# A fused recurrence and gated mixture on one core: 64-bit weights decoded with two VectorE instructions fewer, and the mixture's input splits queued a quarter step later

## The chip, the core and the metric

The kernel runs on one core of a Trainium2 chip. The core has TensorE (PE, matrix products; its weight loads are PEld), VectorE (DVE), ScalarE (ACT) and GpSimd (POOL), each with its own in-order queue, and SyncE (SP), whose queue issues nearly all of the DMAs here. The metric is the device time of one execution in microseconds (us). Times of before are those of three runs and of one profiled execution.

## What is computed

First a recurrence over 768 tokens, for 4 batches and 8 heads with a 40x40 state each; then a mixture over the tokens whose input is the recurrence's output.

```python
for t in range(S):
    y[:, :, t] = np.einsum('bhd,bhde->bhe', rt, state)
    Sa = np.einsum('bhde,bhe->bhd', state, at)
    state_decay = state * wt[:, :, None, :] - np.einsum('bhd,bhe->bhde', Sa, bt)
    state = state_decay + np.einsum('bhd,bhe->bhde', vt, kt)
...
h = np.maximum(x @ w_in, 0.0)
u, v = (h[..., :d_ff // 2], h[..., d_ff // 2:])
v_n = (v - mu) / np.sqrt(var + 1e-06)
v_s = np.einsum('ts,bsd->btd', w_spatial, v_n) + b_spatial[None, :, None]
gated = u * v_s
return (gated @ w_out).astype(np.float32)
```

The arrays `w_in` (320x1024) and `w_out` (512x320) come as 64-bit floats. Products are taken in a reduced fp32 format; to keep their accuracy, each operand is split into a high part and the rest, and three products replace one.

## The kernel before, in words

**Phase 1** is the recurrence in chunks of 64 tokens: two pairs of batches with 12 chunks each make 24 steps (NS = 24). A step handles 8 units in two groups g. Its chain is: `c_bp` (PE, from the state `Mc`) and its eviction on ACT, `c_ff` and its eviction, `c_xx` and its eviction (ACT, then two triangle selects on POOL), `c_mp` (PE) and `c_mp_out` (DVE, line 635), which writes the state for the next step; and `c_y` (PE) with `c_y_out` (DVE, line 659), which frees the PSUM bank that the next `c_bp` writes. Beside it run the preparation of later chunks (two scans and products on DVE, `b_...` products on PE with evictions on ACT and selects on POOL) and, for each group of four chunks, a triangular inversion on DVE in 33 slices (lines 368 and 372).

**The order is written by hand.** `at(t, fn)` puts a call into a list with a time in steps; the list is sorted by that time, then by the order of entry, and all calls before t = 24 are issued in that order. So on each engine the queue is in the order of t. Calls with t of 24 or more, and the whole of phase 2, are ordered by the compiler's planner, which estimates durations; `issue_after` keeps some of them behind marks in phase 1.

**Decoding.** `decode64_steps` (line 57) turns a 128-row tile of 64-bit floats, loaded as pairs of 32-bit words `lo` and `hi`, into the two fp32 parts `h` and `l`. Each `yield` ends a slice. Slice 0 loads; slices 1 to 7 are one DVE instruction each on the words (t[0], t[1], t[2] are three scratch tiles with one buffer each); slice 8 is a copy on ACT that makes `h`; slice 9 is two DVE instructions (lines 98 and 99). `w_in` makes six tiles of 128x512, decoded in steps 4 to 9: tile i has slice k at 4.2 + i + 0.1 k, its load 0.9 earlier (line 858). `w_out` makes four tiles of 128x320, decoded in the last part by `decode64` (line 149).

**The mixture's first half** starts when decoding is over: the decoding scratch is closed at 10.1 and its memory becomes that of the pool `act`. Twelve input tiles of 128 tokens follow, j = 0 to 11. `m_load` (DMAs on SP into the tile `xt`, one buffer), `m_split` (line 697: ACT copies `xt` to `xh`, 128x768; POOL subtracts twice, 128x512 and 64x256), then six products `m_u`/`m_v` in six of the slots of which each step from 11 on has four, at .22, .46, .65 and .80. Here own[0] is a tile's first slot; the tile's load stands at own[0] - 1.6 (10.12 for the first), its split at own[0] - 0.7. So the split of an even j stands at .52 of a step (10.52, 13.52, ...), that of an odd j at .95 (11.95, 14.95, ...).

**Neighbours in the order:** `b_lka_out` at .17 and .19, `c_ff_out` at .34 and .39, `b_l21_out` (line 482) at .54, `c_xx_out` at .60 and .65, `b_zt_out` at .68, `b_h_out` at .72 and .74, `c_mp_out` at .755 and .775, `b_x21_out` at .81, `c_y_out` at .90 and .94, the next step's `c_bp_out` at 1.04 and 1.09.

**Phase 2** is the product with `w_spatial` (lines 184 to 186), the gate (188, 189) and the output product (204). It begins inside the last part of phase 1.

Of the kernel before, what the change touches and what calls it, by code (L numbers as in the profile page):

```python
# [8 lines left out]
F32 = mybir.dt.float32  # L9
# [4 lines left out]
AF = mybir.ActivationFunctionType  # L14
ALU = mybir.AluOpType
# [14 lines left out]
NR = C + E  # L30
LATE = 2 * C
DH = 512

@with_exitstack
def tile_kernel(ctx, tc, early, late, vtok, win, wspT, bsp, wout, out):
    nc = tc.nc
    dram = ctx.enter_context(tc.tile_pool(name="dram", bufs=1, space=DRAM))
    B = out.shape[0]
    S = out.shape[1]
    xs = dram.tile([B, 2, NP, E, S], F32, name="xs")  # L40
    vns = dram.tile([B, S // P, P, DH], F32, name="vns")
    uts = dram.tile([B // NB, S // P, DH // P, P, NB, P], F32, name="uts")
    with ExitStack() as c1:
        marks = phase1(c1, tc, early, late, vtok, win, xs, vns, uts, dram)
    with ExitStack() as c2:
        phase2(c2, tc, marks, vns, uts, wspT, bsp, wout, out)


def split_hi(eng, hi, x):
    eng.activation(hi, x, AF.Copy)  # L50
# [6 lines left out]
def decode64_steps(nc, pool, h, l, src, n, bufs=1):  # L57
    raw = pool.tile([P, n], I64, name="d_raw", bufs=2)
    nc.sync.dma_start(out=raw, in_=src)
    yield  # L60
    words = raw.bitcast(I32).rearrange("p (n two) -> p n two", two=2)
    lo, hi = words[:, :, 0], words[:, :, 1]
    t = [pool.tile([P, n], I32, name=f"d_t{i}", bufs=bufs) for i in range(3)]
    nc.vector.tensor_scalar(
        out=t[0], in0=hi, scalar1=3, scalar2=0x7FFFFFFF,
        op0=ALU.logical_shift_left, op1=ALU.bitwise_and,
    )
    yield
    nc.vector.tensor_scalar(
        out=t[1], in0=hi, scalar1=-0x80000000, scalar2=0x40000000,  # L70
        op0=ALU.bitwise_and, op1=ALU.bitwise_xor,
    )
    yield
    nc.vector.tensor_tensor(out=t[0], in0=t[0], in1=t[1], op=ALU.bitwise_xor)
    yield
    nc.vector.tensor_scalar(
        out=t[1], in0=hi, scalar1=0x7FFFFFFF, scalar2=None, op0=ALU.bitwise_and
    )
    yield
    f1 = t[2].bitcast(F32)  # L80
    nc.vector.scalar_tensor_tensor(
        out=f1, in0=t[1], scalar=float(897 << 20), in1=t[0].bitcast(F32),
        op0=ALU.is_ge, op1=ALU.mult,
    )
    yield
    nc.vector.tensor_scalar(
        out=t[0], in0=t[2], scalar1=-0x800000, scalar2=None, op0=ALU.bitwise_and
    )
    yield
    f2 = t[1].bitcast(F32)  # L90
    nc.vector.scalar_tensor_tensor(
        out=f2, in0=lo.bitcast(U32), scalar=2.0 ** -52, in1=t[0].bitcast(F32),
        op0=ALU.mult, op1=ALU.mult,
    )
    yield
    split_hi(nc.scalar, h, f1)
    yield
    nc.vector.tensor_tensor(out=f1, in0=f1, in1=h.bitcast(F32), op=ALU.subtract)
    nc.vector.tensor_tensor(out=l, in0=f1, in1=f2, op=ALU.add)


def decode64(*args, **kw):
    for _ in decode64_steps(*args, **kw):
        pass


def phase2(ctx, tc, marks, vns, uts, wspT, bsp, wout, out):
    nc = tc.nc

    def behind(*keys):  # L110
        es = ExitStack()
        for key in keys:
            es.enter_context(tc.issue_after(marks[key]))
        return es
# [3 lines left out]
    TH = S // 2  # L118
    ND = DH // P

# [34 lines left out]
    def vload(b):  # L155
        vt[b] = []
        for i in range(NT):
            raw = wstg.tile([P, S], F32, name="raw", bufs=2)[:, 0:DH]
            nc.sync.dma_start(out=raw, in_=vns[b, i])
            vpool = vp[b % 2][i]  # L160
            h = vpool.tile([P, DH], F32R, name=f"vh{b % 2}{i}")
            l = vpool.tile([P, DH], F32R, name=f"vl{b % 2}{i}")
            with behind(("a", 23)):
# [59 lines left out]
def phase1(ctx, tc, early, late, vtok, win, xs, vns, uts, dscr):  # L223
    nc = tc.nc
# [452 lines left out]
    def decode(half, k):  # L677
        cs = slice(half * DH, (half + 1) * DH)
        yield from decode64_steps(nc, st["dec"], wh[:, k, cs], wl[:, k, cs], win[:, k, cs], DH)
# [92 lines left out]
    def at(t, fn, *args):  # L772
        plan.append((t, len(plan), fn, args))
# [60 lines left out]
    for q in range(GS, NS):  # L834
        t = PREP.get(q, q - 8 + 0.01)
# [18 lines left out]
    T_DEC, T_MOE = 4.2, 11  # L854
    for i in range(6):
        gen = decode(1 - i // 3, i % 3)
        for k in range(10):
            at(T_DEC + i + k * 0.10 - (0.9 if k == 0 else 0), step, gen)
    at(T_DEC + 5.9, open_act)
    slots = [T_MOE + k // 4 + (M1, M2, M3, M4)[k % 4] for k in range(3 * NS)]  # L860
# [1 line left out]
    def tail(t):  # L862
        return slots.index(t) if t >= NS else 0

    for j in range(NS // 2):
        bq, i = j // 6, j % 6
        own = slots[6 * j:6 * j + 6]
        at(max(own[0] - 1.6, 2 * j + 2.1, T_DEC + 5.92), m_load, bq, i)
        at(max(own[0] - 0.7, 2 * j + 2.7), m_split, bq, i)
        for t, d in zip((own[0], own[1], own[3], own[4]), range(DH // P)):  # L870
            at(t, m_u, d, bq, i, tail(t))
        for t, g in zip((own[2], own[5]), range(NB)):
            at(t, m_v, g, bq, i, tail(t))
            at(t + 0.14, m_n1, g)
            at(t + 0.42, m_root, g)
            at(t + 0.48, m_n2, g)
            at(t + 0.76, m_n3, g, bq, i)
# [12 lines left out]
    with tc.manual_schedule():  # L890
# [6 lines left out]
        for q in range(P // HB):  # L897
            rows = slice(q * HB, (q + 1) * HB)
            p.affine_select(
                out=maskl[rows], in_=maskl[rows], pattern=[[1, HB]], base=0,  # L900
# [10 lines left out]
        for m, val in ((maskp, 1.0), (maskn, -1.0)):  # L911
            p.memset(m, val)
            for rows in PR:
                p.affine_select(
                    out=m[rows], in_=m[rows], pattern=[[1, C]], base=0,
# [53 lines left out]
        while plan[n][0] < NS:  # L969
            t, _, fn, args = plan[n]  # L970
# [60 lines left out]
```

## Time and profile before

| what | us |
|---|---|
| three runs, median | 671.49 |
| three runs, lowest and highest | 670.7, 673.21 |
| the profiled execution | 672.68 |
| its span, first to last instruction | 671.0 |
| mean granted clock of TensorE, share of full | 0.936 |

The profile lists the execution of one core. "Busy" is the time in which an engine executes. A row of the time line gives start, duration, engine, line of the kernel, operation, output and inputs, count, and in brackets how long the engine had been idle and what released it. A row of the groups gives count, busy time in us, mean of one in ns and the idle time before them. The forty slices give busy tenths; PEclk is the clock that TensorE was granted, in tenths. A row of the windows gives the stretch, its length, the busy time and count of each engine, the granted clock, the share of the DMA engines and GB/s.

By the times of `c_y_out`, step 4 ends at 153.3, step 9 at 246.1, step 10 at 266.6 and step 23 at 496.3 us of the span.

### The profile page before, as it was taken

How to read it: one execution, taken by the hardware profiler on the slowest of the kernel's cores; microseconds unless marked ns; L12 is line 12 of the kernel's file. 1: busy time of each engine (PE TensorE's matmuls, PEld its weight loads, DVE VectorE, ACT ScalarE, POOL GpSimd, SP SyncE). 2: the span in 40 equal slices, each digit the busy share in tenths (PEclk: the TensorE clock that was granted, in tenths of full speed). 3: DMA queues.
4: the chain of work that ended last, by engine and by line, in shares of the span. 5: the costliest groups of instructions: out<-in, count | busy, mean ns of one | idle time of the engine just before them, and what ended most of it. 6: DMA issues, size and time to landing. Idle time of an engine off the chain costs nothing.

```text
span 671.0 us, 25860 instructions
## 1 busy us (share of the span) xinstructions
PE 577.4 (86%) x10960; PEld 522.7 (78%) x10960; DVE 454.1 (68%) x990; ACT 381.0 (57%) x850; POOL 226.5 (34%) x298
## 2 busy tenths in 40 slices
PE   1448784598777888999999999999989999999997
PEld 1347674487666776888888888888879899999997
DVE  7998689979999995878895676453285573322220
ACT  2136662367656665888878887888755552232212
POOL 6013340223232233334342242342243745352121
PEclk9977997679787786999999999999989999999999
DMA  8764866387555546656565256366286467150001
GB/s 190 115 117 66 144 148 136 69 175 147 129 127 122 129 108 125 132 136 170 138 189 153 76 156 168 89 172 162 83 234 191 152 184 231 48 169 30 30 30 59
DMA packets 106331, 87.68 MB, mean 131 GB/s; under 512 B 35496, under 2 KB 92072, under 8 KB 104296
## 3 DMA queue, kind: packets, MB, share of 16 engines
q1 hardware_dynamic: 105672, 84.31, 50.9%
q10 hardware_dynamic: 544, 1.72, 1.2%
q8 instruction: 86, 1.41, 1.0%
q14 instruction: 29, 0.24, 0.1%
HBM read 59.20 MB, written 20.50 MB: 119 GB/s over the span
## 4 chain that ended last, share of the span: by engine, by line
PE 42%; DVE 3%; ACT 2%; DMA 2%; issue 2%; POOL 1%; SPq 0%; ACTq 0%; POOLq 0%; DVEq 0%
PE po L204 6%; PE pg L186 4%; PE pg L185 4%; PE pv L764 4%; PE pg L184 4%; PE pv L717 4%; PE ch L586 2%; PE ch L568 2%; PE bp L550 2%; PE bp L646 1%; PE bk L434 1%; PE bk L456 1%; PE ch L624 1%; DMA vns<-vr 1%; PE bk L404 1%
## 5 line engine op out<-in xcount | busy, mean ns | idle before, releaser
L411 POOL TENSOR_SCALAR_AFFINE_SELECT Rt<-Rt 64x512 f32<-64x512 f32 (+1 forms) x144 | 83.9, 584 | 143.2 <-ACT Rt L597 115.3
L411 POOL TENSOR_SCALAR_AFFINE_SELECT At<-At 64x512 f32<-64x512 f32 x48 | 41.4, 862 | 157.8 <-ACT At L421 153.7
L560 ACT ACTIVATE Rt<-bp 64x416 f32<-64x416 f32 x96 | 49.1, 511 | 49.5 <-PE bp L550 47.8
L188 DVE TENSOR_TENSOR g<-pg,bb 128x384 f32<-128x384 f32 x32 | 17.7, 555 | 79.1 <-PE pg L186 69.5
L368 DVE TENSOR_TENSOR itmp<-A 128x30 f32<-128x30 f32 (+9 forms) x180 | 67.3, 374 | 3.2
L550 PE MATMUL bp<-lin,Mc 40*64 40x104 f32 x768 | 48.2, 284 | 21.7 <-DVE y L659 21.2
L184 PE MATMUL pg<-wsh,vh 128*128 128x384 f32 x192 | 65.0, 339 | 0.0
L185 PE MATMUL pg<-wsl,vh 128*128 128x384 f32 x192 | 65.0, 338 | 0.0
L186 PE MATMUL pg<-wsh,vl 128*128 128x384 f32 x192 | 63.2, 338 | 0.0
L372 DVE TENSOR_TENSOR A<-A,itmp 128x30 f32<-128x30 f32 (+9 forms) x180 | 59.0, 328 | 6.2
L550 PEld LDWEIGHTS bp<-lin,Mc 40*64 40x64 f32 x768 | 42.0, 155 | 24.7 <-DVE y L659 23.8
L54 POOL TENSOR_TENSOR gl<-g,gh 128x384 fp32r<-128x384 f32 x32 | 33.3, 1044 | 59.2 <-ACT gh L50 59.2
L597 ACT ACTIVATE Rt<-ch 64x416 f32<-64x416 f32 x96 | 49.1, 511 | 4.7 <-PE ch L586 2.4
L50 ACT ACTIVATE gh<-g 128x384 fp32r<-128x384 f32 x32 | 16.6, 521 | 53.5 <-DVE g L189 53.5
L568 PE MATMUL ch<-Rt,At 128*64 128x104 f32 x768 | 45.3, 276 | 1.8 <-issue 1.1
L344 PE MATMUL bk<-at,sl 64*32 64x32 f32 x1536 | 21.6, 206 | 26.9 <-DVE sl L329 20.7
L568 PEld LDWEIGHTS ch<-Rt,At 128*64 128x64 f32 x768 | 40.0, 152 | 5.8 <-issue 2.3
L586 PE MATMUL ch<-ffs,xf 64*64 64x104 f32 x768 | 42.2, 263 | 0.0
L344 PEld LDWEIGHTS bk<-at,sl 64*32 64x32 f32 x1536 | 18.2, 117 | 29.9 <-issue 14.7
L635 DVE TENSOR_TENSOR Mc<-ch,scn 104x160 f32<-104x160 f32 x44 | 18.4, 434 | 33.1 <-PE ch L624 20.6
L54 POOL TENSOR_TENSOR vl<-raw,vh 128x512 fp32r<-128x512 f32 x24 | 31.4, 1317 | 24.4 <-ACT vh L50 21.2
L586 PEld LDWEIGHTS ch<-ffs,xf 64*64 64x64 f32 x768 | 37.2, 140 | 1.1
(133 smaller groups left out, 1511.6 us busy)
## 6 DMA issues: line engine op xcount, KB each, us to landing
ein<-in_early SPq DMA_DIRECT2D x108, 129.0 KB
lin<-in_late SPq DMA_DIRECT2D x48, 160.0 KB
At<-at SPq DMA_DIRECT2D x48, 128.0 KB
uts<-ur SPq DMA_DIRECT2D x48, 128.0 KB
vns<-vr SPq DMA_DIRECT2D x24, 256.0 KB
raw<-vns SPq DMA_DIRECT2D x24, 256.0 KB
ut<-uts SPq DMA_DIRECT2D x24, 256.0 KB
Rt<-in_vtok SPq DMA_DIRECT2D x48, 80.0 KB
```

The costliest lines, as they stand in the source:

```text
L54: eng.tensor_tensor(out=lo, in0=x, in1=hi.bitcast(F32), op=ALU.subtract)
L184: nc.tensor.matmul(pg, lhsT=vh[:, dc], rhs=w_h, start=(i == 0), stop=False)
L185: nc.tensor.matmul(pg, lhsT=vh[:, dc], rhs=w_l, start=False, stop=False)
L186: nc.tensor.matmul(pg, lhsT=vl[:, dc], rhs=w_h, start=False, stop=(i == NT - 1))
L368: nc.vector.tensor_tensor(out=tp, in0=A[:, k + 1:, k:k + 1].broadcast_to([P, m, k]), in1=A[:, k:k + 1, 0:k].broadcast_to([P, m, k]), op=AL ...
L372: nc.vector.tensor_tensor(out=A[:, k + 1:, 0:k], in0=A[:, k + 1:, 0:k], in1=tp, op=ALU.add)
L411: nc.gpsimd.affine_select(out=t, in_=t, pattern=[[0, k], [1, C]], base=0, channel_multiplier=-1, compare_op=ALU.is_gt, fill=0.0,)
L550: nc.tensor.matmul(bp[PR[par], q, :], lhsT=Mc[RR[par], n, :], rhs=li[RR[par], n, C:], start=(q == 0), stop=False, skip_group_check=True,)
L560: nc.scalar.activation(Rt[par][PR[par], gp, :], st["bp", g][PR[par]], AF.Copy)
L568: nc.tensor.matmul(ff[PR[1 - par], q, :], lhsT=At[par][:, n, :], rhs=Rt[par][:, n, :], start=True, stop=True,)
L586: nc.tensor.matmul(xx[ev, q, :], lhsT=xf[ev, n, :], rhs=ffs[ev, q, :], start=True, stop=True,)
L597: done = nc.scalar.activation(Rt[par][PR[par], gp], xx[PR[1 - par]], AF.Copy, scale=-1.0)
```

## The change

In the decode, four instructions on the high word (shift and mask; keep and flip the sign and top exponent bits; combine; absolute value) become three: a shift and mask that also clears one bit more, a combined and-or on DVE, and an absolute value on ACT, taken of the word read as an fp32 number. The threshold of the comparison on line 82 is then an fp32 constant. DVE has seven instructions per tile instead of nine, ACT two instead of one. The absolute value shares slice 1 with the first DVE instruction, so that a tile has 8 slices instead of 10: the ACT copy is slice 6 instead of 8 (0.2 steps earlier), the closing pair slice 7 instead of 9. Second, every `m_split` stands at own[0] - 0.45 instead of own[0] - 0.7: at .77 of a step for even j, at .20 of the next for odd j.

```diff
+TINY = 1.125 * 2.0 ** -15
...
     nc.vector.tensor_scalar(
-        out=t[0], in0=hi, scalar1=3, scalar2=0x7FFFFFFF,
+        out=t[0], in0=hi, scalar1=3, scalar2=0x3FFFFFFF,
         op0=ALU.logical_shift_left, op1=ALU.bitwise_and,
     )
+    nc.scalar.activation(t[1].bitcast(F32), hi.bitcast(F32), AF.Abs)
     yield
-    nc.vector.tensor_scalar(
-        out=t[1], in0=hi, scalar1=-0x80000000, scalar2=0x40000000,
-        op0=ALU.bitwise_and, op1=ALU.bitwise_xor,
-    )
-    yield
-    nc.vector.tensor_tensor(out=t[0], in0=t[0], in1=t[1], op=ALU.bitwise_xor)
-    yield
-    nc.vector.tensor_scalar(
-        out=t[1], in0=hi, scalar1=0x7FFFFFFF, scalar2=None, op0=ALU.bitwise_and
+    nc.vector.scalar_tensor_tensor(
+        out=t[0], in0=hi, scalar=-0x40000000, in1=t[0], op0=ALU.bitwise_and, op1=ALU.bitwise_or,
     )
     yield
     f1 = t[2].bitcast(F32)
     nc.vector.scalar_tensor_tensor(
-        out=f1, in0=t[1], scalar=float(897 << 20), in1=t[0].bitcast(F32),
+        out=f1, in0=t[1].bitcast(F32), scalar=TINY, in1=t[0].bitcast(F32),
         op0=ALU.is_ge, op1=ALU.mult,
     )
...
         gen = decode(1 - i // 3, i % 3)
-        for k in range(10):
+        for k in range(8):
             at(T_DEC + i + k * 0.10 - (0.9 if k == 0 else 0), step, gen)
...
-        at(max(own[0] - 0.7, 2 * j + 2.7), m_split, bq, i)
+        at(max(own[0] - 0.45, 2 * j + 2.7), m_split, bq, i)
```

## The prediction

> **What bounds the kernel now.** I read the engines' busy line and the forty slices first, then the windows by stage, then the time line of VectorE (DVE) and of ScalarE (ACT) inside the stage that the change touches.
>
> ```profile
> DVE  7998689979999995878895676453285573322220
> ...
> PEclk9977997679787786999999999999989999999999
> ```
>
> A slice is 16.8 us, and the first is slice 0. TensorE (PE) is the busiest engine over the span, but the slices show stages: DVE has nine tenths or more from slice 9 to 14, and the granted clock of PE is mostly at 0.6 to 0.8 there and full later. All six decodes of the expansion weights lie in that part (steps 4 to 9). The windows by stage make it exact (length, then busy time of PE, PEld, DVE, ACT, POOL, granted clock, DMA share, GB/s):
>
> ```profile
> 143.65:257.54 113.89, 90.66 (x2469) 80.53 (x2468) 109.34 (x223) 74.33 (x169) 34.13 (x49) 0.88 0.58 130
> ...
> 257.54:267.10 9.56, 9.28 (x233) 7.92 (x234) 3.20 (x9) 5.23 (x12) 4.81 (x8) 0.50 0.87 140
> ...
> 257.54:484.00 226.46, 224.52 (x4965) 194.53 (x4966) 147.23 (x371) 179.69 (x404) 78.59 (x120) 0.98 0.54 140
> 484.00:545.00 61.00, 56.89 (x407) 51.99 (x404) 37.69 (x103) 33.91 (x73) 29.31 (x28) 0.97 0.60 182
> ```
>
> From 143.65 to 257.54 DVE is busy 109.34 of 113.89 us while ACT has 74.33. Then PE is busy for 224.52 of 226.46 us. So a microsecond taken from DVE before 257.5 should move everything behind it, and one taken later, nothing. DVE's time line shows where that run begins and ends:
>
> ```profile
> 143.19 0.42 DVE L354 TENSOR_TENSOR Lc<-bk,maskl 128x256 f32<-128x256 f32 x1 [2.17 <-PE bk L344]
> ...
> 149.20 0.45 DVE L635 TENSOR_TENSOR Mc<-ch,scn 104x160 f32<-104x160 f32 x1 [1.29 <-ACT Rt L597]
> 150.04 0.44 DVE L635 TENSOR_TENSOR Mc<-ch,scn 104x160 f32<-104x160 f32 x1 [0.40 <-PE ch L624]
> ...
> 262.02 0.44 DVE L635 TENSOR_TENSOR Mc<-ch,scn 104x160 f32<-104x160 f32 x1 [4.13 <-DMA Rt<-in_vtok]
> ```
>
> Between 150.04 and the 4.13 us of idle time before 262.02 no row of DVE has a wait in brackets: its queue is never empty for over 100 us.
>
> **Part 1: two DVE instructions fewer per decode (steps 4 to 9).** Lines 69, 74 and 76 go, one SCALAR_TENSOR_TENSOR over the same 128x512 words comes. In a full queue an instruction costs the time from its start to the next start; tile 1:
>
> ```profile
> 163.65 0.42 DVE L69 TENSOR_SCALAR d_t<-d_raw 128x512 int32<-128x512 int32 x1
> 163.99 0.58 DVE L368 TENSOR_TENSOR itmp<-A 128x210 f32<-128x210 f32 x1
> ...
> 164.90 0.69 DVE L74 TENSOR_TENSOR d_t<-d_t,d_t 128x512 int32<-128x512 int32 x1
> 165.50 0.84 DVE L368 TENSOR_TENSOR itmp<-A 128x220 f32<-128x220 f32 x1
> ...
> 166.68 0.45 DVE L76 TENSOR_SCALAR d_t<-d_raw 128x512 int32<-128x512 int32 x1
> 167.05 0.38 DVE L368 TENSOR_TENSOR itmp<-A 128x228 f32<-128x228 f32 x1
> ```
>
> Removed: 0.34 + 0.60 + 0.37 = 1.31 us. The new instruction is not in the trace; the nearest row is line 91's, of the same kind and size, which reads every other word as it will. The last row of this view is ScalarE's copy of the same tile, for later:
>
> ```profile
> L74 DVE TENSOR_TENSOR d_t<-d_t,d_t 128x512 int32<-128x512 int32 x6 | 4.3, 710 | 0.0
> ...
> L91 DVE SCALAR_TENSOR_TENSOR d_t<-d_raw,d_t 128x512 f32<-128x512 uint32 x6 | 4.1, 681 | 0.0
> ...
> L76 DVE TENSOR_SCALAR d_t<-d_raw 128x512 int32<-128x512 int32 x6 | 3.0, 497 | 0.0
> L69 DVE TENSOR_SCALAR d_t<-d_raw 128x512 int32<-128x512 int32 x6 | 2.8, 468 | 0.0
> ...
> L50 ACT ACTIVATE wh<-d_t 128x512 fp32r<-128x512 f32 x6 | 3.8, 630 | 4.1 <-DVE d_t L81 4.1
> ```
>
> It lasts 681 ns; less the 0.08 us or so by which an instruction overlaps the next (0.69 against 0.60 above) it is 0.61 us. Net per tile 0.70 us from below. By the means of the rows it is 468 + 710 + 497 - 681 = 994 ns. I take 0.8 for five tiles, 4.0. Tile 0 falls into step 4, where DVE still waits (the first three rows of its time line), so its removed instructions only lengthen those waits; but the generator is shorter, so two of its other instructions (lines 86 and 91, 0.34 + 0.60) now come ahead of the wait that ends at 149.20. I count 0.6. **Sum 4.6 us; bounds 3.5 (0.70, tile 0 at nothing) and 5.6 (0.994, tile 0 at 0.6).**
>
> The two bounds differ because some of the rows are stretched while GpSimd works. In step 20 this is plain: the TENSOR_SCALAR of line 76 over 128x320 words lasts 1.29 us beside a split's subtraction on POOL, and 0.33 where POOL is idle.
>
> ```profile
> 448.10 1.29 DVE L76 TENSOR_SCALAR d_t<-d_raw 128x320 int32<-128x320 int32 x1
> ...
> 489.99 0.33 DVE L76 TENSOR_SCALAR d_t<-d_raw 128x320 int32<-128x320 int32 x1
> ...
> 446.48 2.73 POOL L54 TENSOR_TENSOR xl<-xt,xh 128x512 fp32r<-128x512 f32 x1 [2.53 <-DMA Rt<-in_vtok]
> ```
>
> The Trainium skill, "SBUF — State Buffer", section "SBUF: two separate sides", says that VectorE and GpSimd share one port pair as an exclusive lock that whoever starts first holds for its whole instruction. The rows agree. By that rule the stretch is met by whichever DVE instruction comes next, the new one with two SBUF inputs too, so the removal would be worth the lower 0.70 per tile, and part 1 some 4.1 us.
>
> **What becomes late instead.** The steps' own chain is next: y (L659) of one step, through bp, ff, xx and the state product (L624), to DVE's L635 of the next.
>
> ```profile
> 227.49 0.41 DVE L659 TENSOR_TENSOR y<-bp,Et 104x256 f32<-104x256 f32 x1
> ...
> 239.79 0.51 PE L624 MATMUL ch<-tk,Rt 128*40 128x40 f32 x16
> ...
> 242.93 0.78 DVE L635 TENSOR_TENSOR Mc<-ch,scn 104x160 f32<-104x160 f32 x2
> ```
>
> From the end of the second y (227.90) the chain takes 12.4 us (to 240.30), DVE 15.0 (to 242.93). In the new order the closing pair (lines 98 and 99, 1.3 us) stands ahead of the second y instead of behind it, and line 91 ahead of L635: DVE's side becomes some 15.0 - 1.3 + 0.3 = 14.0, the chain's 12.4 plus the new ACT instruction. That leaves about 1 us per step: enough, but no more.
>
> **The absolute value on ScalarE.** It is queued in front of c_ff_out. Nothing shows it on this engine; the nearest row is the copy of the tile, 630 ns, and the DVE run leaves ACT 113.89 - 74.33 = 39.6 us idle, 6 us a step. I take 0.63 on ACT and nothing on the end; if the 1 us of slack were gone, 6 x 0.63 = 3.8 us. Behind it wait c_ff_out, tok_out and then PE's c_xx; ahead of it, its data (a DMA issued 0.9 steps earlier) and the previous tile's last use of the buffer (0.4 steps earlier) are done. The four output decodes, of 128x320 words, lie in the last part, where DVE is busy 37.69 and ACT 33.91 of 61.00 us: they save and cost nothing there by themselves.
>
> **Part 2: the split, 0.25 steps later.** Step 10 holds the first one:
>
> ```profile
> 252.93 1.13 ACT L781 ACTIVATE xf<-XT 128x256 f32<-128x256 f32 x3
> 256.43 0.84 ACT L50 ACTIVATE xh<-xt 128x768 fp32r<-128x768 f32 x1 [2.37 <-DMA xt<-xs]
> 257.30 0.78 ACT L482 ACTIVATE l<-bk 32x256 f32<-32x256 f32 x2
> 258.10 2.12 ACT L597 ACTIVATE Rt<-ch 64x416 f32<-64x416 f32 x4
> ...
> 253.41 1.64 PE L586 MATMUL ch<-ffs,xf 64*64 64x104 f32 x32
> 257.73 1.46 PE L492 MATMUL bk<-XT,l 32*32 32x32 f32 x32 [2.67 <-ACT l L482]
> ...
> 264.22 1.94 PE L646 MATMUL bp<-Rt,tk 128*40 128x64 f32 x32
> ...
> 237.15 2.12 ACT L597 ACTIVATE Rt<-ch 64x416 f32<-64x416 f32 x4
> ...
> 240.85 1.09 PE L646 MATMUL bp<-Rt,tk 128*40 128x64 f32 x32
> ```
>
> ACT is free at 254.06, waits 2.37 us for the input tile, copies it for 0.84, and only then evicts what PE has had ready since 255.05. At 10.77 instead of 10.52 the split stands behind c_xx_out, zt_out and h_out. L482 could start at 254.06: **3.2 us.** PE's 2.67 us of idle time goes with it, and that matters twice: the window from 257.54 to 267.10 runs at a granted clock of 0.50. In step 9, at full clock, the evictions' end (239.27) to c_y's end (241.94) takes 2.7 us; here 260.22 to 266.16, 5.9. If the clock stays up, another 3.2 us; in step 8 too an idle time of 2.5 us is followed by half clock:
>
> ```profile
> 226.99 2.52 PE L550 MATMUL bp<-lin,Mc 40*64 40x104 f32 x26 [2.53 <-DVE y L659]
> ...
> 228.00:230.00 2.00, 2.00 (x40) 0.50 0.62 150
> ```
>
> (The second row is a window of PE alone.) I take **2.0** (bounds 0 and 3.2).
>
> All twelve splits move, each one ACT and two POOL instructions, no DMA: on ACT past c_xx_out, zt_out and h_out or past c_bp_out and lka_out, on POOL past the triangle selects. The DMAs of the next input wait in SP's queue for the split's release, now 0.28 steps behind it instead of 0.53: about 4.9 us (226.46 us over 13 steps, 17.4 each). All eight POOL instructions of the window from 257.54, the split's two among them, take 4.81, so SP may wait a microsecond, and the input copies behind it with it. In the PE-bound stage only 226.46 - 224.52 = 1.9 us are there to win; I count 0, bounds a gain of 1.9 and a loss of 1. The tenth split leaves the order written by hand (23.95 becomes 24.20) and the four output decodes change, so the last part's order, which a planner makes, will change: 61.00 - 56.89 = 4.1 us of PE idle time are there to win and as much to lose; I count 0.
>
> **Sum:** 4.6 + 3.2 + 2.0 = 9.8 us. The profiled execution took 672.68 (span 671.0 and 1.7 around it), so 662.9; the three runs' median is 671.49, 1.2 below it, so **661.7 us**.
>
> **Rivals.** (1) *The new wait eats the old one's place*: the chain's slack is less than 1 us, steps 5 to 9 gain nothing and pay the 0.63 on ACT; the split's 3.2 + 2.0 remains: -5.2 + 3.8 = -1.4, 670.1. Against it: 12.4 against 14.0. Chance 0.10. The Trainium skill, "ScalarE: Activation LUTs", section "Rules for kernel authors", would have simple elementwise work on VectorE rather than ScalarE; by that rule this rival wins. The rows bear it out in size only (630 ns on ACT against 497 or less on DVE); DVE is the full engine here. (2) *The last part's new order gives back* 4 us: 665.7. For it: PE stands idle there now for 4.1 us. Chance 0.18. (3) *Slower: function tables.* The one load in the trace serves all 850 activations:
>
> ```profile
> L253 ACT ACT_TABLE_LOAD x1 | 1.3, 1283 | 1.4 <-PEq L1018 1.4
> ```
>
> Were the absolute value in another table, ten uses would bring twenty loads of 1.28 us, 25.7 us on ACT; less 6 us of slack in steps 4 to 9, and with 9.8 won, about +10: 681. It decides from eight loads on the path. Chance 0.04. The same page, section "Table sets: the hidden batching unit", lists abs among the cheap functions that every set holds; no row here shows it. (4) *More*: the clock stays up in steps 5 to 9 as well and the last part tightens, another 5 us: 656.5. Chance 0.08.
>
> **Numbers.** Forecast (657.5 to 665) 0.55, rival 2 with half successes up to 668 0.20, rival 1 and other small outcomes 0.13, rival 4 0.08, slower 0.04. A change below 0.5% (3.4 us) could not be told from none: faster 0.83, same 0.13, slower 0.04. The range, 655.5 to 669.0, spans from rival 4 to almost rival 1.
>
> **What would show it.** Right: the DVE run ends 4 to 5 us earlier (near 253); ACT's L482 of step 10 follows L781 without a wait; no half clock after it; PE's dense stage begins 8 to 11 us earlier and stays as long; one table load. Wrong: waits in brackets on L635 or L659 in steps 5 to 9, ACT idle for a function table, or a last part longer than 61 us.

## The result, and the profile after

| kernel | median, us | lowest, highest | runs | ratio to the kernel before, 95% interval |
|---|---|---|---|---|
| before | 671.49 | 670.46, 677.24 | 5 | |
| changed | 664.92 | 659.76, 670.56 | 5 | 0.9865 [0.9825, 0.9906] |

The change gains 6.6 us by the medians of all runs; the forecast was 9.8 (661.7 us). The ratio leaves out the slow run of the changed kernel (670.56) and stands for 9.1 us, with an interval from 6.3 to 11.8, so the five runs of each kernel don't tell the gain from the forecast. The profiled execution of the changed kernel took 665.08 us (span 663.3), 7.6 less than that of before.

Where the time went is read from `c_y_out`, whose second row in a step ends the step. The steps' lengths in the two profiles:

| stage | before | changed | difference |
|---|---|---|---|
| up to the end of step 3 (same instructions) | 135.5 | 134.2 | -1.3 |
| steps 4 to 9 | 110.6 | 107.6 | -3.0 |
| step 10 | 20.6 | 13.7 | -6.9 |
| step 11 | 16.3 | 22.4 | **+6.0** |
| steps 12 to 22 | 198.7 | 197.3 | -1.4 |
| step 23 and the rest | 189.3 | 188.2 | -1.1 |

Two stages gain as forecast in sign. Step 11 gives most of step 10's gain back.

The window of before from the end of step 3 to the end of step 9 (length, busy time of PE, PEld, DVE, ACT, POOL, granted clock, DMA share, GB/s):

```profile
135.46:246.07 110.61, 90.41 (x2502) 80.50 (x2502) 104.24 (x213) 72.08 (x163) 33.16 (x48) 0.87 0.60 133
```

The same of the changed kernel, then its step 10, and the dense stage behind step 11:

```profile
134.19:241.75 107.56, 88.48 (x2502) 78.29 (x2502) 101.72 (x203) 74.99 (x169) 34.12 (x48) 0.89 0.61 136
...
241.66:255.14 13.48, 12.63 (x401) 11.16 (x398) 12.93 (x29) 11.52 (x27) 5.50 (x9) 1.00 0.45 121
...
279.40:476.00 196.60, 195.66 (x4325) 169.69 (x4321) 127.89 (x332) 161.25 (x364) 67.77 (x104) 1.00 0.53 142
```

DVE's busy time falls by 2.5 us and so does the stage, by 3.0; ACT has 6 instructions and 2.9 us more. Step 10 runs at full clock. The dense stage of PE behind it stays dense: 195.66 of 196.60 us.

The groups of the changed kernel (count, busy us, mean ns, idle before):

```profile
L318 DVE TENSOR_TENSOR at<-ein,Et 128x512 f32<-128x512 f32 x7 | 6.6, 941 | 0.2
...
L71 DVE SCALAR_TENSOR_TENSOR d_t<-d_raw,d_t 128x512 int32<-128x512 int32 x6 | 4.1, 685 | 0.0
L65 DVE TENSOR_SCALAR d_t<-d_raw 128x512 int32<-128x512 int32 x6 | 3.4, 571 | 0.0
L81 DVE TENSOR_SCALAR d_t<-d_t 128x512 int32<-128x512 int32 x6 | 3.0, 498 | 0.0
...
L69 ACT ACTIVATE d_t<-d_raw 128x512 f32<-128x512 f32 x6 | 4.0, 674 | 0.0
...
L248 ACT ACT_TABLE_LOAD x1 | 1.3, 1283 | 1.4 <-PEq L1013 1.4
```

The new DVE instruction takes 685 ns (681 taken in the forecast), the absolute value 674 (630 taken), and there is still one table load. The same view of before has the rows of the same three instructions shorter (of line 64 only the mask has changed):

```profile
L323 DVE TENSOR_TENSOR at<-ein,Et 128x512 f32<-128x512 f32 x6 | 4.4, 735 | 0.2
...
L86 DVE TENSOR_SCALAR d_t<-d_t 128x512 int32<-128x512 int32 x6 | 2.7, 446 | 0.0
L64 DVE TENSOR_SCALAR d_t<-d_raw 128x512 int32<-128x512 int32 x6 | 2.5, 418 | 0.0
```

The time line of the changed kernel in step 10 and the start of step 11, ACT and PE:

```profile
247.21 1.13 ACT L776 ACTIVATE xf<-XT 128x256 f32<-128x256 f32 x3
248.36 0.78 ACT L477 ACTIVATE l<-bk 32x256 f32<-32x256 f32 x2
...
253.94 0.84 ACT L51 ACTIVATE xh<-xt 128x768 fp32r<-128x768 f32 x1 [0.78 <-issue]
...
261.99 0.58 PE L563 MATMUL ch<-Rt,At 128*64 128x104 f32 x2 [3.42 <-issue]
263.68 3.00 PE L563 MATMUL ch<-Rt,At 128*64 128x104 f32 x30 [1.12 <-DMA Rt<-in_vtok]
```

Line 477 follows line 776 at once: the wait for the input tile is gone. But 6.6 us after step 10 has ended (255.42), `c_ff` (line 563) is only beginning: PE stands for 3.42 and, after two products, for 1.12 us, the second time for `Rt<-in_vtok`, the token rows that `vtok_load` brings in two transfers (due at .48 and .62 of the step before). The bracket of the first wait names nothing, but it is the first transfer: the trace has the last updates of the two transfers' semaphores at 261.90 and 263.55 us, each 0.1 us before the products that follow. The clock pays too: over 264 to 266 us the window shows

```profile
264.00:266.00 2.00, 2.00 (x28) 2.00 (x25) 2.00 (x2) 0.52 (x1) 0.00 (x0) 0.50 0.45 120
```

a granted clock of 0.50 with PE busy throughout. The reason is in SP's queue, the same time line:

```profile
241.44 1.56 SPq L666 DMA_DIRECT2D xs<-y  x4
...
255.46 0.60 SPq L384 DMA_DIRECT2D Rt<-in_vtok  x1
...
257.08 0.58 SPq L384 DMA_DIRECT2D Rt<-in_vtok  x1
```

From the storing of step 9's output at 241.44 to the second issue of token rows at 257.08 SP works through 23 transfers, at about 0.6 us an issue, almost without a gap: 15.6 us. In before the list is as long, but step 10 took 20.6 us and `c_ff` of step 11 began 10.6 us after the issue:

```profile
245.76 1.57 SPq L671 DMA_DIRECT2D xs<-y  x4
...
260.02 0.57 SPq L389 DMA_DIRECT2D Rt<-in_vtok  x1
...
270.64 1.65 PE L568 MATMUL ch<-Rt,At 128*64 128x104 f32 x32
```

By the same semaphore the rows had landed there at 266.30, 4.3 us before their use. Now step 10 takes 13.7, less than the list, and PE asks for the rows some 1.5 us after their issue (it is out of other work at 258.57); they land 6.5 us after it, about as long as in before (6.3).

### The profile page after: what moved, and what is told of

Same layout as the page of the kernel before. It is cut to its first block, busy times and chain, and to the rows that moved or that the text cites. A ratio compares the mean times of both kernels' runs of the same rounds, so it can differ in the third digit from the quotient of the medians.

```text
span 663.3 us, 25848 instructions
## 1 busy us (share of the span) xinstructions
PE 571.8 (86%) x10960; PEld 518.3 (78%) x10960; DVE 448.4 (68%) x970; ACT 384.2 (58%) x860; POOL 225.9 (34%) x298
## 4 chain that ended last, share of the span: by engine, by line
PE 63%; DVE 15%; DMA 7%; issue 6%; ACT 4%; SPq 3%; POOL 1%; DVEq 0%; ACTq 0%; POOLq 0%
PE po L199 6%; PE pv L759 6%; PE pv L712 6%; PE pg L179 5%; PE pg L180 5%; PE pg L181 5%; PE ch L563 4%; PE bp L545 4%; PE ch L581 4%; PE bk L429 2%; DMA ein<-in_early 2%; DVE itmp L363 2%; PE bk L451 2%; PE bk L399 2%; PE bp L641 2%
## 5 line engine op out<-in xcount | busy, mean ns | idle before, releaser
L563 PE MATMUL ch<-Rt,At 128*64 128x104 f32 x768 | 48.0, 283 | 5.9 <-issue 4.8
L563 PEld LDWEIGHTS ch<-Rt,At 128*64 128x64 f32 x768 | 42.2, 157 | 10.4 <-issue 7.1
L339 PE MATMUL bk<-at,sl 64*32 64x32 f32 x1536 | 21.2, 203 | 26.5 <-DVE sl L324 20.7
L339 PEld LDWEIGHTS bk<-at,sl 64*32 64x32 f32 x1536 | 17.7, 114 | 29.5 <-issue 14.4
L179 PEld LDWEIGHTS pg<-wsh,vh 128*128 128x128 f32 x192 | 36.6, 190 | 2.4 <-ACT vh L51 2.2
L630 DVE TENSOR_TENSOR Mc<-ch,scn 104x160 f32<-104x160 f32 x44 | 18.5, 436 | 29.0 <-PE ch L619 18.7
```

Source lines behind the costliest of these rows:

```text
L179: nc.tensor.matmul(pg, lhsT=vh[:, dc], rhs=w_h, start=(i == 0), stop=False)
L563: nc.tensor.matmul(ff[PR[1 - par], q, :], lhsT=At[par][:, n, :], rhs=Rt[par][:, n, :], start=True, stop=True,)
```

## The experiments

The kernels ran in three groups, each group on one chip together with the kernel before, whose medians there were 670.33 us (split_only, decode_only, first_split, vtok_early), 673.07 (after_again, vtok_again, decode_again, abs_twice) and 672.63 (vtok_third, vtok_abs_dve, before_vtok, before_again). The stages of all profiles, in us, for the readings below:

| kernel | up to step 3 | steps 4-9 | step 10 | step 11 | 12-22 | 23 and rest |
|---|---|---|---|---|---|---|
| before | 135.5 | 110.6 | 20.6 | 16.3 | 198.7 | 189.3 |
| before_again | 136.5 | 110.6 | 20.7 | 16.3 | 199.2 | 188.1 |
| split_only | 136.9 | 111.6 | 15.2 | 17.3 | 196.4 | 189.7 |
| decode_only | 135.3 | 110.4 | 20.3 | 16.4 | 198.4 | 187.4 |
| decode_again | 135.9 | 110.2 | 21.2 | 16.3 | 198.3 | 188.1 |
| changed | 134.2 | 107.6 | 13.7 | 22.4 | 197.3 | 188.2 |
| after_again | 135.5 | 108.7 | 14.7 | 16.9 | 197.6 | 186.5 |
| abs_twice | 136.3 | 109.6 | 13.9 | 21.0 | 197.7 | 187.5 |
| first_split | 139.4 | 107.5 | 15.0 | 16.2 | 198.4 | 186.9 |
| vtok_early | 137.6 | 109.1 | 13.7 | 15.4 | 199.2 | 186.3 |
| vtok_again | 138.0 | 107.3 | 13.7 | 15.4 | 198.4 | 188.2 |
| vtok_third | 136.7 | 107.6 | 13.7 | 15.4 | 199.6 | 189.2 |
| vtok_abs_dve | 136.2 | 112.9 | 14.8 | 15.8 | 198.6 | 191.4 |
| before_vtok | 138.1 | 110.1 | 21.1 | 15.9 | 199.4 | 188.4 |

The first column is a measure of the scatter: nothing but the early token rows touches it, and it takes 134.2 to 139.4 us.

### Each part alone: split_only, decode_only, decode_again

The kernel before with the later splits only:

```diff
-        at(max(own[0] - 0.7, 2 * j + 2.7), m_split, bq, i)
+        at(max(own[0] - 0.45, 2 * j + 2.7), m_split, bq, i)
```

> The old nine-instruction decode with all splits 0.25 steps later. Theory (a new wait, step 11's token rows from the DMA queue, eats what step 10 wins): step 10, which took 20.6 us from the end of one y to the next and 13.7 with both changes, is held by VectorE's run to 257.5 and comes to 15 to 16; then the first product of step 11 waits some 2 us for the token rows, and the whole gains 3 to 5 us. Rival (the two parts are independent and add, the wait in step 11 belongs to the pair): step 10 falls by the full 6.9 us and the whole by 6 to 7.

Measured: 667.94 us (664.05 to 674.3, 12 runs), ratio 0.9955 [0.9936, 0.9974]. Step 10 falls by 5.4 us, to 15.2, as the theory said. Most of the rest of the way to 13.7 is the clock: at the start of the step PE had stood 3.87 us for the last y of step 9, as its time line shows, and the 26 products of line 550 take 2.52 us, where the next step has 1.38 for as many at full clock. In step 11 the second transfer of token rows is awaited for 0.82 us, not 2; the bracket names an eviction into `ur`, which `c_ff` doesn't read, but the last update of the rows' semaphore is at 268.52 us.

```profile
248.19 2.52 PE L550 MATMUL bp<-lin,Mc 40*64 40x104 f32 x26 [3.87 <-DVE y L659]
...
268.65 1.61 PE L568 MATMUL ch<-Rt,At 128*64 128x104 f32 x30 [0.82 <-ACT ur L766]
```

The whole gains 2.4 us by the medians and 3.0 by the ratio, about the lower end of the theory's 3 to 5; the rival's 6.9 and 6 to 7 us didn't come.

The changed kernel with the splits put back (0.45 to 0.7), that is, the shorter decoding alone:

> The new decode with the splits where they were. Theory: VectorE's run ends 3 to 4.5 us earlier; ScalarE still waits for the input tile in step 10, TensorE still idles and drops to half clock, step 10 stays at 19 to 21 us, and step 11 has no wait for token rows (about 16.3 us). Whole: 3 to 4.5 us faster than before. Rival (the decode's gain is the one that is eaten): less than 1.5 us. If the parts' gains add to more than the 6.6 us that both brought, they share a bound.

Measured: 668.46 us (665.72 to 673.5, 12 runs), ratio 0.9989 [0.9962, 1.0016]; steps 4 to 9 as long as before, step 10 still 20.3 us. The gain, 1.9 us by the medians and 0.7 by the ratio, is nearer to the rival's than to the theory's. Its step 5 held a wait of 3.21 us of PE; in most other profiles it is 0.6 to 2.2. So it ran again:

> The shorter decoding alone, once more. Theory A (the shorter decoding is worth 2 to 3 us in steps 6 to 9 by itself, and the 3.2 us in which TensorE stood in step 5 came from one execution): steps 4 to 9 take 107.2 to 108.6 us, step 10 still 20 us with ScalarE standing at the split, ratio to the kernel before 0.995 to 0.997. Theory B (a faster VectorE by itself runs into the loads of the early rows): step 5 takes over 20 us again and the ratio stays within 0.2% of 1.

Measured: 669.27 us (666.91 to 673.63, 12 runs), ratio 0.9946 [0.9915, 0.9977]. The ratio is near theory A's; steps 4 to 9, at 110.2 us, are not, and step 5 at 19.5 lies between: neither theory's numbers hold together. Up to step 10 this kernel's order is the changed kernel's on every engine, so that its 110.2 and 110.4 and the 107.5 to 108.7 of changed, after_again and first_split are one order's scatter. Its step 10 keeps the old wait and the half clock; ACT's row:

```profile
257.06 0.84 ACT L51 ACTIVATE xh<-xt 128x768 fp32r<-128x768 f32 x1 [3.27 <-DMA xt<-xs]
```

By the medians on the same chip the decoding alone gains 1.9 and 3.8 us and the split 2.4: together 4.3 to 6.2, with 6.6 and 7.9 for both at once (changed and after_again). By the ratios it is 0.7 and 3.6, 3.0, and 9.1 and 7.9. The parts add up to less than the pair each time; the intervals, 1.3 us and more to each side, neither show nor exclude that the pair gains more than its parts.

### The token rows earlier: vtok_early, vtok_again, vtok_third

The changed kernel with the token rows queued ahead of the input tile's loads:

```diff
-            at(q - 1 + 0.48 + 0.14 * par, vtok_load, q, par)
+            at(q - 1 + 0.03 + 0.01 * par, vtok_load, q, par)
```

> The changed kernel, with each step's token rows queued 0.45 to 0.58 steps earlier on SyncE, ahead of the mixture's input tiles. Theory: in step 11 the first product (c_ff) no longer waits (3.42 and 1.12 us) nor drops to half clock, step 11 falls from 22.4 to 16.5 to 17.5 us, and the whole gains 4 to 6 us on the changed kernel: about 659 to 661. Rival (the DMA engines, not the order of the queue, are full between 256 and 262 us, and another transfer is late instead): step 11 stays above 20 us and the whole gains less than 2.

> The changed kernel with the token rows queued 0.45 of a step earlier, once more beside the changed kernel. Theory A: steps 10 and 11 take 28.5 to 30 us together again, ratio to the kernel before 0.984 to 0.988, 0.4 to 0.7% below after_again. Theory B: as after_again within 0.2%.

> The changed kernel with the token rows queued 0.45 of a step earlier, as the base for vtok_abs_dve: 660.5 to 663.5 us, steps 4 to 9 in 107 to 109 us, steps 10 and 11 in 29.1 us together for the third time.

Measured: 661.44 us (659.97 to 663.01), 662.45 (660.68 to 664.64) and 663.31 (660.53 to 667.54), 6 runs each; ratios 0.9866 [0.984, 0.9892], 0.9851 [0.9812, 0.9891], 0.9844 [0.9793, 0.9894]. In all three profiles step 10 takes 13.7 and step 11 15.4, less than the theory's 16.5 to 17.5; the rival is dead. vtok_third's windows of the two steps:

```profile
244.28:257.94 13.66, 12.81 (x406) 11.34 (x403) 13.11 (x29) 11.39 (x26) 5.36 (x9) 1.00 0.52 131
257.94:273.35 15.41, 15.41 (x341) 13.67 (x337) 14.30 (x26) 10.68 (x24) 6.17 (x10) 1.00 0.73 141
```

PE is busy for all of step 11, at full clock. This is the fastest version, 8.9 to 10.6 us below the kernel before on the same chip. On the second chip it stands 2.7 us below the changed kernel (662.45 to 665.17), though the two intervals overlap. Not all of step 11 is gained: the table has 0.7 to 2.3 us more in steps 12 to 22 than for the changed kernel. Step 3 ended at 136.7 to 138.0 us (changed: 134.2 and 135.5), but without the early rows it ended as late in first_split.

### The changed kernel again: after_again

> The changed kernel as it is, once more. Theory A (the token rows' transfer is always the last thing to arrive in step 11, since step 10 is now shorter than the list of transfers that the sync engine issues in front of it): the profile shows TensorE waiting 3 to 5 us for it in step 11 again, step 11 takes 20 to 23 us, and the kernel is 0.4 to 0.7% slower than vtok_again. Theory B (the wait was one execution's accident): step 11 takes 15 to 17 us and the two kernels agree within 0.2%.

Measured: 665.17 us (661.28 to 667.83, 6 runs), ratio 0.9882 [0.9838, 0.9927]. Step 11 takes 16.9 us, as theory B said, and not theory A's 20 to 23. Yet the rows are awaited again, for 0.78 us at the same product: the bracket names the eviction into `ur`, but the last update of the rows' semaphore is at 263.37 us. So theory A was right that they come last and wrong on how much. By the medians vtok_again is 0.4% faster, as theory A said, but the two intervals overlap; and this profiled execution (661.69 us) is the second fastest of six, so a longer wait in the slower ones is neither seen nor excluded. The profile also has half clock in step 10, here its windows:

```profile
242.00:244.00 2.00, 0.40 (x19) 0.29 (x20) 1.97 (x5) 0.00 (x0) 0.00 (x0) 0.62 0.03 8
244.00:246.00 2.00, 2.00 (x24) 2.00 (x26) 1.93 (x6) 0.36 (x1) 0.00 (x0) 0.50 0.43 122
```

PE stood 1.89 and 1.60 us around one short group at the end of step 9. At half clock step 10 takes 14.7 us instead of 13.7, so `c_ff` of step 11 asks a microsecond later; SP's list is also 1.2 us shorter this time (14.4 us from the store at 243.85). The time line has the rows almost in time:

```profile
258.29 0.58 SPq L384 DMA_DIRECT2D Rt<-in_vtok  x1
...
262.34 0.39 PE L563 MATMUL ch<-Rt,At 128*64 128x104 f32 x2
263.51 1.61 PE L563 MATMUL ch<-Rt,At 128*64 128x104 f32 x30 [0.78 <-ACT ur L761]
```

So it is a race whose outcome changes from execution to execution. In the five profiles with the later first split and the rows at their old place, PE waits for the rows each time: 4.5 us in the changed kernel, 3.5 in abs_twice, 0.8 in after_again and split_only, 0.1 in first_split; they land 4.9 to 6.8 us after the second issue. After a step 10 of 13.7 to 13.9 us the wait is long, after one of 14.7 to 15.2 short; so either way the 6.9 us of step 10 aren't all kept.

### Only the first split later: first_split

```diff
-        at(max(own[0] - 0.45, 2 * j + 2.7), m_split, bq, i)
+        at(max(own[0] - (0.7 if j else 0.45), 2 * j + 2.7), m_split, bq, i)
```

> The changed kernel with only the first split 0.25 steps later, the other eleven as before. Theory (the other splits lie in the stage that TensorE fills): steps 12 to 22 together within 1.5 us of the changed kernel's 197.3, the whole within 2 us of it. Rival (moving the others off c_xx_out or c_bp_out is worth something at each): steps 12 to 22 longer by 3 us or more.

Measured: 665.71 us (663.67 to 670.02, 10 runs), ratio 0.9946 [0.992, 0.9972]. Steps 4 to 11 gain as with all splits moved; half clock again in step 10, next to no wait in step 11 (0.07 us). Steps 12 to 22 take 198.4 us, as in before (198.7, 199.2), while the changed kernel has 197.3 and 197.6 and split_only 196.4: within the theory's 1.5 us of 197.3, and the rival's 3 us are dead. So the other splits are worth 1 to 2 us in the profiles, of 1.9 us that the forecast held to be possible and counted at nothing. By the ratio the kernel gains 3.6 us (1.9 to 5.4) where the pair gains 9.1 and 7.9 on other chips; the eleven may be worth more than the profiles show, and where isn't seen.

### What the absolute value costs: abs_twice, vtok_abs_dve

The changed kernel with the absolute value issued twice on ACT, in the six decodings and, since they share the code, in the four output decodings too:

```diff
-    nc.scalar.activation(t[1].bitcast(F32), hi.bitcast(F32), AF.Abs)
+    for _ in range(2):
+        nc.scalar.activation(t[1].bitcast(F32), hi.bitcast(F32), AF.Abs)
```

> The changed kernel with ScalarE's absolute value issued twice, a second 0.67 us of ScalarE in each of the six decodings. Theory A (ScalarE has room in steps 4 to 9, so its new instruction costs nothing): steps 4 to 9 take 107.5 us within 0.6, and the time agrees with after_again within 0.2%. Theory B (VectorE waits for ScalarE in the decoding): steps 4 to 9 take 4 us longer, since 6 times 0.67 us are added, and the time is 0.5 to 0.7% above after_again.

Measured: 667.64 us (663.91 to 672.72, 12 runs), ratio 0.9922 [0.9886, 0.9958]; steps 4 to 9 in 109.6 us, step 11 with the wait. By the stage it is 2.0 us above the changed kernel and 0.9 above after_again, by the medians 2.5: between the theories, and within one order's scatter. A row in step 8 shows the way in which it could cost; PE waits for an eviction that stands behind the absolute values on ACT:

```profile
218.29 0.69 PE L469 MATMUL bk<-sl,at 64*32 64x32 f32 x32 [1.31 <-ACT tk L458]
```

With a single absolute value the same wait reaches 2.29 us (after_again, 179.09), with none 0.93 (split_only); what it costs in the end is open.

vtok_early with the absolute value back on DVE, eight instructions a tile, in all ten decodings:

```diff
-    nc.scalar.activation(t[1].bitcast(F32), hi.bitcast(F32), AF.Abs)
+    nc.vector.tensor_scalar(
+        out=t[1], in0=hi, scalar1=0x7FFFFFFF, scalar2=None, op0=ALU.bitwise_and
+    )
```

> As vtok_third, but VectorE takes the absolute value itself (the masking instruction of the kernel before, 0.42 to 0.5 us), so eight VectorE instructions a decoding and none more on ScalarE. Theory A (VectorE is the only bound of steps 4 to 9, ScalarE's instruction is free): six times 0.5 are added, steps 4 to 9 take 3 us longer and the kernel is 0.4 to 0.5% above vtok_third. Theory B (what ScalarE took over comes back as waits for ScalarE, which is why the decoding gave half of the 4.6 us): steps 4 to 9 take as long as in vtok_third within 1 us, and the times agree within 0.2%.

Measured: 670.94 us (666.98 to 676.03, 12 runs), ratio 0.9971 [0.9942, 1.0]: 7.6 us above vtok_third, more than both theories, which had overlooked the output decodings. The instruction itself is 415 ns, six of them 2.5 us; the four of the output decodings take another 2.4, one of them 1.29 us. Steps 6 to 9 take 72.8 us instead of 71.0, 0.47 a step, about its duration. The rest comes in lumps, two of them on PE's time line:

```profile
156.21 0.86 PE L341 MATMUL bk<-at,sl 64*32 64x32 f32 x48 [3.79 <-issue]
...
248.81 2.52 PE L547 MATMUL bp<-lin,Mc 40*64 40x104 f32 x26 [3.37 <-DVE y L656]
```

The first wait was 1.47 us in vtok_third (step 5: 21.8 us to 19.0); after the second, step 10 runs at half clock for 1.1 us more; and step 23, where two of the four stand, takes 17.6 instead of 14.9 (step 23 and the rest together 2.2 us more). Theory B is dead: taking the absolute value off ACT gained nothing. Why the lump of step 5 changes so much isn't settled; the profile names no releaser for it.

### The kernel before with early token rows, and once more as it was: before_vtok, before_again

The edit of vtok_early, on the kernel before:

> The kernel before with the token rows queued 0.45 of a step earlier and nothing else. Theory A (in the kernel before this transfer lands long before it is needed; the change made it late): no gain, ratio to the kernel before 0.998 to 1.002, step 11 in 15.4 to 16.4 us. Theory B (the earlier token rows are worth 3 us to any version): ratio 0.995 to 0.996. In both, steps 4 to 9 take 110 to 112 us, with the old decoding.

> The kernel before, once more, for a second profile of it. If its profile was typical: steps 4 to 9 take 110 to 112 us, step 10 takes 20 to 21 us with ScalarE standing at the split for 2 to 2.5 us, step 11 takes 16 to 17 us with no wait for the token rows.

Measured: before_vtok 678.59 us (674.62 to 683.39, 12 runs), ratio 1.0074 [1.0041, 1.0106]; before_again's one run 673.14. The earlier token rows are worth 2.7 us to the changed kernel, by medians whose intervals overlap, and cost the kernel before 5.0 us by the ratio and 6.0 by the medians: neither theory allowed for that. The time line of before_vtok in step 10 shows the direction:

```profile
259.59 0.84 ACT L50 ACTIVATE xh<-xt 128x768 fp32r<-128x768 f32 x1 [3.60 <-DMA xt<-xs]
...
260.89 0.24 PE L492 MATMUL bk<-XT,l 32*32 32x32 f32 x2 [3.90 <-ACT l L482]
```

Its counterpart in before_again:

```profile
257.65 0.84 ACT L50 ACTIVATE xh<-xt 128x768 fp32r<-128x768 f32 x1 [2.53 <-DMA xt<-xs]
258.95 1.46 PE L492 MATMUL bk<-XT,l 32*32 32x32 f32 x32 [2.83 <-ACT l L482]
```

The token rows now stand in front of the input tile's loads, and there the split still waits for exactly those loads: 1.1 us longer. This profiled execution was the fastest of its twelve; where the other runs lost 4 us more wasn't seen. before_again confirms the profile of before to 0.2 us in steps 4 to 11.

## Why the prediction was right, and where it was not

**The time and the direction** were right: 664.92 us in a range of 655.5 to 669.0, 6.6 us gained of 9.8 by the medians and 9.1 by the ratio. Some of that is luck: part 1 came out smaller, part 2 larger, and step 11 lost what nobody had counted.

**Part 1, 4.6 us: right in mechanism, too large.** The removed rows were worth what the forecast said: the means of a tile's decoding rows add up to 5.34 us in before and 4.58 after, 0.75 a tile and 4.5 for six. But `at` (line 318) went from 735 to 941 ns, 1.2 us in six, because it now often meets a select on GpSimd (in step 8 it starts at 229.4 us, and two selects run from 229.33 to 231.04; its median was 691 ns and is 953). In DVE's busy time 2.5 us remain, with two instructions more in the stage by the counts (213 to 203, where 12 went). The four profiles with the old decoding average 110.7 us in steps 4 to 9, the eight with the new one and a single absolute value on ACT 108.5: **2.2 us**. Much of the scatter lies in step 5; steps 6 to 9 alone take 73.5 us before and 71.7 after, 0.44 us a tile against the 0.8 forecast. Tile 0's 0.6 us can't be seen: step 4 takes 17.3 to 19.0 us before and 17.6 to 18.5 after. Of the bounds 3.5 to 5.6 the lower one was too high: they priced how long the removed rows were, but not that the stretch by GpSimd moves on to another row. Nor did VectorE's run end near 253, as the forecast's sign had it: without the wait of step 10 DVE has no wait between 149.05 and 274.01 us.

The Trainium skill's exclusive lock ("SBUF — State Buffer", section "SBUF: two separate sides") was read in the prediction to say that the next DVE instruction takes over the stretch. That is the direction of line 318, a product of two SBUF inputs; the 4.1 us worked out from it were still too many.

**What becomes late in steps 5 to 9: nothing**, as forecast. No row of lines 630 or 654 waits there, and rival 1 is dead. The absolute value on ACT was priced at nothing; the twofold one leaves room for up to 2.5 us, unsettled.

**Part 2, 3.2 + 2.0 us: right, and the second term too small.** Step 10 fell by 6.9 us, and by 5.4 with the split alone. The 3.2 is the wait in front of line 482, which is gone. Of the clock's 0 to 3.2 I took 2.0. What step 10 lost beyond the 3.2 is 3.7 where the clock stays up (13.7 us), more than the upper bound, and 2.2 to 2.7 where an earlier wait brings half clock (14.7 to 15.2); which of them comes differs between two executions of the changed kernel. The bound had left out that step 10 of before runs at half clock near its start too, behind a wait of 2.20 us at 245.79 (0.50 from 248 to 250 us); in after_again such a spell costs 1.0.

The Trainium skill, "TensorE: Matmul & The Clock Gate", section "What's actually happening", has the clock fall after an idle window of about 3.4 us that runs free of the kernel's own beat. Standing times of 3.87 us (split_only) and 3.49 in two pieces (after_again) brought it here, and so had 2.53 in before. That 2.53 is enough speaks against a full window of idleness. The delay changes, which agrees with the free-running part: behind the 2.53 us of before the same 26 products take 2.52 us, behind a longer gap in vtok_third 1.51, and half clock comes a microsecond later, as two windows (of all engines) show:

```profile
227.99 1.51 PE L545 MATMUL bp<-lin,Mc 40*64 40x104 f32 x26 [3.06 <-DVE A L367]
...
228.00:230.00 2.00, 2.00 (x48) 2.00 (x50) 1.93 (x4) 0.95 (x2) 0.00 (x0) 0.77 0.49 98
230.00:232.00 2.00, 2.00 (x36) 1.88 (x32) 1.97 (x4) 1.88 (x5) 0.14 (x1) 0.50 0.71 155
```

A gap of 2.29 us in after_again (at 179.09) left the clock at 1.00.

**The step that failed** is "SP may wait a microsecond, and the input copies behind it with it". It named SP's queue, but weighed only what the split holds up. It did not ask what 7 us less in step 10 do to a list of transfers that takes 14 to 16 us to issue. In before the token rows had landed 4.3 us ahead of their use, less than the 6.9 us that step 10 lost; step 11 lost 6.0 us in the changed kernel's profile and 0.6 in after_again's. So the dense stage of PE behind step 11 began 5.2 us earlier in the span (277.8 against 283.0), not 8 to 11. With the rows queued earlier the sum comes out: 8.9, 10.6 and 9.3 us against the 9.8 forecast. That agreement owes something to offsetting errors: part 1 came out smaller, the clock larger, and steps 10 and 11 together gained 7.8 us (36.9 to 29.1).

**The other eleven splits, 0:** 1 to 2 us gained in the profiles, about the bound of 1.9; the times of first_split leave room for more. **The last part, 0:** step 23 and the rest take 186.5 and 188.2 us after, 189.3 and 188.1 before: no change that can be told. Rival 2 (4 us given back in the last part) had nearly the right time, 665.7, for the wrong place. **Rival 3** is dead (one table load). **Rival 4** (all of it better by 5 us, which makes 656.7 and not 656.5) didn't come.

## What to carry to other kernels

When a stage gets shorter, go through every queue that feeds the next one and ask of each transfer how long before its use it lands: a list of transfers that was hidden by the old wait becomes the new one as soon as the stage loses more than that. The best place in a transfer queue belongs to the version: the same move of one load gained some 3 us here after the change and cost 5 to 6 before it. And take two or three profiles before a stage's difference is believed: the same instructions in the same order took 107.5 to 110.4 us in steps 4 to 9.

## What the runs showed that was not expected

- Issuing is a resource of its own: SP needed 0.6 us for each of the transfers between one step's output and the next token rows, 14.3 to 15.6 us in all, longer than step 10 without waits (13.7).
- A fast step can be followed by a slow one and a slow step by a fast one (13.7 and 22.4; 14.7 and 16.9), both of the same kernel: half clock in step 10 and a quicker SP gave the transfer most of the time that it lacked.
- One DVE instruction more in each of ten tiles, 4.9 us in all, cost 7.6 us by the medians; in the profiles the lumps are a longer wait in step 5, half clock in step 10, and 2.7 us in step 23. That the instruction brings the lumps was not tested.
